# Letting any free flexible PSUM bank serve as the third bank of a ScalarE slot, and up to two VectorE jobs ride in one row-tiled score visit

## The chip, the cores and the metric

The kernel runs on one core of one Trainium2 chip. The metric is device time in microseconds (us); lower is better. Each timed run also lists the mean granted TensorE clock of the core (1.0 is full speed). Ratios are the mean time of one kernel's fast runs over the mean time of the other kernel's fast runs of the same rounds on the same chip, with a 95% interval. They are therefore not quite the ratios of the medians that are quoted beside them.

## The reference

A layernormed input goes through a 32-head softmax attention and through a gated unit, and the two are multiplied and added to the input:

```python
x = A_x                                      # (1, 2048, 640) bf16
xn = layernorm(x)
# attention, 32 heads of 20
q, k, v = split(xn @ wqkv)
p = softmax(einsum("bhqd,bhkd->bhqk", q, k) * 20 ** -0.5)
s = einsum("bhqk,bhkd->bhqd", p, v) @ wo
# gated unit, F = 1728
h = sigmoid(xn @ w_gate) * (xn @ w_up)
g = silu(h @ w_down)
return x + s * g
```

The attention has 32 x 2048 x 2048 scores. The kernel handles them as 2048 score tiles of 128 x 512 (8 groups of 4 heads, 4 query chunks, 16 key tiles, 4 heads each).

## The kernel before

A score tile needs an exponential. Two engines share that work. ScalarE takes most tiles, in "slots": two tiles lie in a two-bank PSUM tile (`scA`) and are done in one instruction, and a third may lie in a flexible bank (`bk`), as an instruction of its own. VectorE takes the others with integer arithmetic: one conversion per tile out of PSUM (`iv`), then three passes over a group of four tiles (`pb`). TensorE makes the scores in "visits" (heads of 20 rows are padded to 32 rows, a quarter of the array, so up to four score matmuls of different heads run at once; in the timeline below three start within 0.01 us), multiplies the finished tiles by V ("PV"), and fills the rest of its time with projections and the gated unit ("M"). Those M items need a flexible bank too. There are only three flexible banks.

All orders are fixed when the program is built. A small list scheduler with a clock of its own walks through time in steps of 0.02 us and decides what each engine issues next. On the chip every engine runs its list in order, so a late instruction holds up all that stands behind it (below, one output projection that waits 1.94 us holds up a score visit).

```python
# exponentials of a slot on ScalarE
m = len(jobs)
if m == SLOT:                                     # SLOT = 3
    flex[nexp % 2] = now + t_exp(1) + EL          # the slot's OWN flexible bank comes free
    exp_act(pt[:, 2, :], bank[nexp % 2])
exp_act(pt[:, 0:min(m, 2), :], scA[nexp % 2][:, 0:min(m, 2), :])
...
# a score visit on TensorE
d_bank, own = None, nfill % 2
if d_can and busy <= T_F + T_MODE + PL + SLACK:   # VectorE's backlog is small enough
    d_bank = next((f for f in [...][D_ORD] if flex[f] <= now), None)
want = SLOT if flex[nfill % 2] <= now and d_bank != nfill % 2 else SLOT - 1
... # at most one job for VectorE
jobs = claim_act(want, d_new[2][2] if d_new else None)
...
# output projections may start when a normalized block is expected to have landed
norm_b(*tm[1:])
o_at[tm[1]] = now + 11.5
```

## Time and profile before

Three runs took 839.08 to 841.6 us, median 841.25. The profiled run has a span of 839.8 us.

The first two lines below are from the profile's page of the kernel before: the busy time of each engine, and the granted TensorE clock in 40 slices of the span (9 is 90% or more). The next line is the chain of waits that ended last, by engine. The last two are groups of instructions (each shape apart): line, engine, operation, tiles, shapes and count, then busy time and mean ns of one, then the engine's idle time before them and what ended it.

```profile
PE 788.4 (94%) x6354; PEld 278.5 (33%) x6411; DVE 765.4 (91%) x1194; ACT 796.0 (95%) x1003; POOL 77.5 (9%) x84
...
PEclk9999999999999999999999999999999999999998
...
ACT 49%; PE 28%; DVE 13%; issue 6%; DMA 2%; SPq 1%; POOL 0%; POOLq 0%; ACTq 0%; DVEq 0%
...
L80 ACT ACTIVATE pt<-scA 128x1024 bf16<-128x1024 f32 x719 | 715.3, 1160 | 4.6 <-PE bk L860 2.9 <-PE scA L860 1.0
L80 ACT ACTIVATE pt<-bk 128x512 bf16<-128x512 f32 x129 | 94.5, 733 | 4.0 <-PE bk L860 3.8
```

Three engines are over 90% busy, so busy shares do not say who bounds the kernel. The chain does: ScalarE holds half of it. The mean of one exponential (1160 ns) is not its cost, because activations are pipelined and their records overlap.

The cost is the distance between starts. The next ScalarE instruction starts 903 ns after a 128x1024 exponential at best, 476 ns after a 128x512 one, 316 ns after a 128x320 tanh. Throughout this document, "ScalarE's sum" is all its instructions between the first and the last exponential times these best distances, and a "stall" is what a distance has above its best. (Four tanhs of 64x512 in each kernel are counted at 476 ns, though none takes under 612: 0.5 us of every kernel's stalls is this.) The stage from first to last exponential is the sum plus the stalls. (The prediction starts the stage one instruction later, at 34.0 us, hence its 777.6 and 754.2 us.)

| before | us |
|---|---|
| stage (33.5 to 811.7 us) | 778.1 |
| ScalarE's sum | 754.6 |
| stalls before 50 us / 50 to 755 us / after 755 us | 0.2 / 20.7 / 2.6 |
| behind the last exponential's start | 28.1 |

TensorE in the middle of the stage looks like this (timeline of the kernel before; columns are start, duration, engine, line, operation, tiles, shapes, count):

```profile
301.62 0.39 PE L860 MATMUL scA<-q,kT 32*128 32x512 bf16 x2
301.63 0.39 PE L860 MATMUL bk<-q,kT 32*128 32x512 bf16 x1
301.94 0.39 PE L897 MATMUL oacc<-pt,v 128*21 128x512 bf16 x2
301.95 0.39 PE L897 MATMUL oacc<-pb,v 128*21 128x512 bf16 x2
302.27 0.39 PE L641 MATMUL bk<-xnT,wgu 128*128 128x512 bf16 x1
302.60 0.39 PE L860 MATMUL scA<-q,kT 32*128 32x512 bf16 x2
302.60 0.39 PE L860 MATMUL bk<-q,kT 32*128 32x512 bf16 x1
```

A visit with two tiles for ScalarE and one for VectorE, one PV round, one M step and the next visit start about 0.32 us apart. Within one kind of work it is 0.213 us, so a change of kind costs about 0.107 us.

### The profile page before, as it was taken

How to read it: one execution, taken by the hardware profiler on the slowest of the kernel's cores; microseconds unless marked ns; L12 is line 12 of the kernel's file. 1: busy time of each engine (PE TensorE's matmuls, PEld its weight loads, DVE VectorE, ACT ScalarE, POOL GpSimd, SP SyncE). 2: the span in 40 equal slices, each digit the busy share in tenths (PEclk: the TensorE clock that was granted, in tenths of full speed). 3: DMA queues.
4: the chain of work that ended last, by engine and by line, in shares of the span. 5: the costliest groups of instructions: out<-in, count | busy, mean ns of one | idle time of the engine just before them, and what ended most of it. 6: DMA issues, size and time to landing. Idle time of an engine off the chain costs nothing.

```text
span 839.8 us, 16932 instructions
## 1 busy us (share of the span) xinstructions
PE 788.4 (94%) x6354; PEld 278.5 (33%) x6411; DVE 765.4 (91%) x1194; ACT 796.0 (95%) x1003; POOL 77.5 (9%) x84
## 2 busy tenths in 40 slices
PE   4799999999999999999999999999999999999995
PEld 2432323333333323333333233333233322333342
DVE  7789899999899998998999999999998988999994
ACT  7799999999999999999999999999999999999970
POOL 5000000000000001000000000000000000002333
PEclk9999999999999999999999999999999999999998
DMA  5711212123222132213121232131311223111642
GB/s 154 205 51 50 60 51 49 47 57 82 72 62 63 43 85 69 68 44 82 52 61 53 68 85 67 45 92 49 109 65 46 66 71 78 28 47 57 193 147 91
DMA packets 92979, 62.21 MB, mean 74 GB/s; under 512 B 34648, under 2 KB 86408, under 8 KB 92896
## 3 DMA queue, kind: packets, MB, share of 16 engines
q1 hardware_dynamic: 92608, 60.79, 25.7%
q8 instruction: 50, 0.82, 0.4%
q10 hardware_dynamic: 288, 0.33, 0.1%
q14 instruction: 33, 0.27, 0.1%
HBM read 46.24 MB, written 12.39 MB: 70 GB/s over the span
## 4 chain that ended last, share of the span: by engine, by line
ACT 49%; PE 28%; DVE 13%; issue 6%; DMA 2%; SPq 1%; POOL 0%; POOLq 0%; ACTq 0%; DVEq 0%
ACT pt L80 44%; PE scA L860 8%; PE oacc L897 5%; DVE iv L1194 5%; PE bk L679 4%; PE bk L641 3%; ACT tnh L80 3%; DVE pb L951 2%; PE bk L765 2%; PE bk L504 2%; DVE pb L945 1%; DVE pb L948 1%; DMA ld<-on 1%; PE psk L140 1%; ACT td L80 1%
## 5 line engine op out<-in xcount | busy, mean ns | idle before, releaser
L80 ACT ACTIVATE pt<-scA 128x1024 bf16<-128x1024 f32 (+1 forms) x729 | 720.2, 1153 | 4.6 <-PE bk L860 2.9
L1194 DVE TENSOR_SCALAR iv<-bk 128x512 int16<-128x512 f32 x471 | 318.6, 682 | 31.7 <-PE bk L860 30.2
L860 PE MATMUL scA<-q,kT 32*128 32x512 bf16 x1448 | 282.6, 382 | 16.7 <-ACT pt L80 9.6
L860 PE MATMUL bk<-q,kT 32*128 32x512 bf16 x600 | 215.5, 383 | 2.0 <-DVE iv L1194 1.7
L897 PE MATMUL oacc<-pt,v 128*21 128x512 bf16 x1577 | 183.1, 382 | 0.6 <-ACT pt L80 0.3
L860 PEld LDWEIGHTS <-kT 32*128 32x128 bf16 x2048 | 88.7, 91 | 261.6 <-issue 246.8
L897 PE MATMUL oacc<-pb,v 128*21 128x512 bf16 x942 | 152.9, 382 | 1.8 <-DVE on L910 1.5
L951 DVE TENSOR_TENSOR pb<-iv,pb 128x2048 bf16<-128x2048 bf16 x118 | 146.8, 1244 | 0.8
L641 PE MATMUL bk<-xnT,wgu 128*128 128x512 bf16 x471 | 142.6, 383 | 3.6 <-issue 1.7
L927 POOL TENSOR_TENSOR on_bf<-on,rl 128x512 bf16<-128x512 f32 x30 | 43.3, 1443 | 692.7 <-DMA rl<-rd 326.0
L80 ACT ACTIVATE pt<-bk 128x512 bf16<-128x512 f32 x129 | 94.5, 733 | 4.0 <-PE bk L860 3.8
L945 DVE TENSOR_SCALAR pb<-iv 128x2048 int16<-128x2048 int16 x118 | 86.3, 731 | 2.5
L679 PE MATMUL bk<-wd,hT 128*128 128x320 bf16 x448 | 86.9, 302 | 1.2 <-DVE iv L1194 0.7
L948 DVE TENSOR_SCALAR pb<-iv 128x2048 int16<-128x2048 int16 x118 | 82.6, 700 | 0.0
L897 PEld LDWEIGHTS <-v 128*21 128x21 bf16 x2519 | 50.4, 90 | 92.2 <-issue 69.4
L641 PEld LDWEIGHTS <-wgu 128*128 128x128 bf16 x520 | 37.1, 97 | 66.2 <-issue 50.4
L679 PEld LDWEIGHTS <-hT 128*128 128x128 bf16 x448 | 34.4, 97 | 48.4 <-issue 39.4
L504 PE MATMUL bk<-xnT,wu 128*120 128x512 bf16 x160 | 49.3, 399 | 0.4 <-DVE iv L1194 0.3
L80 ACT ACTIVATE tnh<-bk 128x512 bf16<-128x512 f32 (+1 forms) x56 | 41.6, 742 | 0.1
L649 DVE SCALAR_TENSOR_TENSOR hT<-tnh,bk 128x512 bf16<-128x512 bf16 x52 | 35.3, 680 | 5.9 <-PE bk L641 5.2
L612 PE MATMUL bk<-wv,xnT 128*128 128x160 bf16 x280 | 29.2, 234 | 0.7 <-ACT pt L80 0.6
L612 PEld LDWEIGHTS <-xnT 128*128 128x128 bf16 x280 | 18.6, 98 | 14.4 <-issue 14.1
(116 smaller groups left out, 381.3 us busy)
## 6 DMA issues: line engine op xcount, KB each, us to landing
wgu<-in_B_w_gate_dram SPq DMA_DIRECT2D x24, 320.0 KB
wgu<-in_B_w_up_dram SPq DMA_DIRECT2D x24, 320.0 KB
rl<-rd SPq DMA_DIRECT2D x120, 64.0 KB
gq_dram<-gqs SPq DMA_DIRECT2D x32, 160.0 KB
xnT<-gq_dram SPq DMA_DIRECT2D x12, 320.0 KB
xt<-in_A_x_dram SPq DMA_DIRECT2D x16, 160.0 KB
wd<-in_B_w_down_dram SPq DMA_DIRECT2D x1, 2080.0 KB
oU<-on_bf SPq DMA_DIRECT2D x104, 20.0 KB
```

Source lines behind the costliest of these rows:

```text
L80: return nc.scalar.add_instruction(mybir.InstActivation(func=func, name=nc.get_next_instruction_name(), engine=ENG.Activation, ins=[nc.sca ...
L504: nc.tensor.matmul(st["ps"][0:UC, :], lhsT=wus[u][:, kd, i, :], rhs=xnT[:, c, kd, :], start=(kd == 0), stop=(kd == KD - 1))
L612: nc.tensor.matmul(st["ps"][:, i * 2 * GC:(i + 1) * 2 * GC], lhsT=xn_tok(tts[i], kd), rhs=wvs[pr][:, kd, :], start=(kd == 0), stop=(kd == ...
L641: nc.tensor.matmul(st[key][0:fs, :], lhsT=w[:, i, kd, ko * P:ko * P + fs], rhs=xnT[:, c, kd, :], start=(kd == 0), stop=(kd == KD - 1))
L679: nc.tensor.matmul(st["ps"][:, 0:HD], lhsT=hT[0:fsz[kf], kf, t4 * P:(t4 + 1) * P], rhs=wd[0:fsz[kf], kf, h * HD:(h + 1) * HD], start=(kf = ...
L860: nc.tensor.matmul(dst, lhsT=kTs[(b // NQC) % 2][32 * j:32 * j + 32, kt * P:(kt + 1) * P], rhs=qts[b % 3][32 * j:32 * j + 32, :], start=Tr ...
L897: nc.tensor.matmul(oacc[32 * j:32 * j + DH + 1, :], lhsT=lhsT, rhs=u["src"], start=first, stop=last, tile_position=(0, 32 * j), skip_group ...
L927: nc.gpsimd.tensor_tensor(out=on_bf, in0=on, in1=rl, op=ALU.mult)
L945: nc.vector.tensor_scalar(out=pb[:, 0, :, :].bitcast(I16), in0=iv, scalar1=0x7F80, scalar2=1, op0=ALU.bitwise_and, op1=ALU.bitwise_or)
L948: nc.vector.tensor_scalar(out=pb[:, 1, :, :].bitcast(I16), in0=iv, scalar1=0x007F, scalar2=0x3F00, op0=ALU.bitwise_and, op1=ALU.bitwise_or)
L951: nc.vector.tensor_tensor(out=pb[:, 1, :, :], in0=iv.bitcast(BF16), in1=pb[:, 1, :, :], op=ALU.mult)
L1194: nc.vector.tensor_scalar(out=d["iv"][:, j, :], in0=bank[bk], scalar1=B_OFF, scalar2=0.0, op0=ALU.add, op1=ALU.max)
```

## The change

The intent is to make score visits fuller, so that TensorE needs fewer of them and changes its kind of work less often. Any free flexible bank may now be the third bank of a slot, and one visit may carry two VectorE jobs. Cut to its core:

```diff
+D_MAX, SLACKS = 2, (0.2, 0.2)
+A_BANKS, D_BANKS = ((0, 1, 2), (1, 0, 2)), ((2, 1, 0), (2, 1, 0))
+M_BANKS = ((2, 1, 0), (2, 1, 0))
...
-                                flex[nexp % 2] = now + t_exp(1) + EL
+                                flex[s["third"]] = now + t_exp(1) + EL
-                                exp_act(pt[:, 2, :], bank[nexp % 2])
+                                exp_act(pt[:, 2, :], bank[s["third"]])
...
-                    if d_can and busy <= T_F + T_MODE + PL + SLACK:
-                        d_bank = next((f for f in [...][D_ORD] if flex[f] <= now), None)
-                    want = SLOT if flex[nfill % 2] <= now and d_bank != nfill % 2 else SLOT - 1
+                    while len(d_new) < D_MAX and (dcur is not None or buf_free(iv_left, NIV)) \
+                            and busy + T_IV * len(d_new) <= T_F + T_MODE + PL + SLACKS[len(d_new)]:
+                        f = next((f for f in D_BANKS[own] if flex[f] <= now), None)
+                        ...                                    # claim a job for bank f
+                    third = next((f for f in A_BANKS[own] if flex[f] <= now), None) if len(d_new) < 2 else None
+                    jobs = claim_act(SLOT if third is not None else SLOT - 1, [y[2][2] for y in d_new])
```

(The line that prefers to wait 0.4 us for a bank and the bank order of M items were adapted too.) Because a scheduler sits between this and the program, the diff does not say what moves. The built orders of instructions do:

| | before | after |
|---|---|---|
| score visits / changes of TensorE's kind of work | 731 / 1530 | 691 / 1443 |
| exponentials of 128x1024 / in a third bank / 128x512 from scA | 719 / 129 / 10 | 686 / 210 / 2 |
| tiles on ScalarE / VectorE | 1577 / 471 | 1584 / 464 |
| PV visits | 665 | 670 |

More of the change, by code (lines that the diff above doesn't have):

```diff
@@ L840, in claim_act @@
             while len(got) < n:
-                js = [j for j in range(GH) if left[b][j] and j != not_j and all(x[2] != j for x in got)]
+                js = [j for j in range(GH) if left[b][j] and j not in not_j and all(x[2] != j for x in got)]
                 if not js:
@@ L848, in claim_act, with claim_dve @@
         return got
-    def claim_dve(had):
+    def claim_dve(had, not_j):
         for b in range(base(), min(NBLK, base() + 2)):
@@ L854, in claim_dve @@
             if n_left[b] >= (D_LAST if b < NBLK - 1 else D_LAST_END):
-                return take(b, max((j for j in range(GH) if left[b][j]),
-                                   key=lambda j: (j not in had, len(left[b][j]), j)), -1)
+                js = [j for j in range(GH) if left[b][j] and j not in not_j]
+                return take(b, max(js, key=lambda j: (j not in had, len(left[b][j]), j)), -1) if js else None
         return None
@@ L1249 @@
                         behind = done < due() + LAG
-                        for f in ((2,) if not behind and claimed[0] < NJOB * NBLK and not (FALL and not pv_ok and not can_f) else [(2, 1 - own, own), (2, own, 1 - own)][M_ORD]):
+                        for f in ((2,) if not behind and claimed[0] < NJOB * NBLK and not (FALL and not pv_ok and not can_f) else M_BANKS[own]):
                             if flex[f] <= now:
@@ L1268 @@
                     nxt = "PV"
-                elif can_f and (margin < URGENT or (stay is None and not (flex[nfill % 2] <= now + WAIT3 and flex[nfill % 2] > now and margin > WAIT3))):
+                elif can_f and (margin < URGENT or (stay is None and not (margin > WAIT3 and any(now < flex[f] <= now + WAIT3 for f in A_BANKS[nfill % 2]) and not any(flex[f] <= now for f in A_BANKS[nfill % 2])))):
                     nxt = "F"
@@ L1279 @@
                 if nxt == "F":
-                    d_can = dcur is not None or buf_free(iv_left, NIV)
                     busy = max(0.0, free["DVE"] - now) + T_IV * len(dq)
-                    d_bank, own = None, nfill % 2
-                    if d_can and busy <= T_F + T_MODE + PL + SLACK:
-                        d_bank = next((f for f in [(2, 1 - own, own), (2, own, 1 - own), (own, 2, 1 - own)][D_ORD] if flex[f] <= now), None)
-                    want = SLOT if flex[nfill % 2] <= now and d_bank != nfill % 2 else SLOT - 1
@@ L1286 @@
-                    d_new = None
-                    if d_bank is not None:
-                        x = claim_dve([t[2] for t in dcur["jobs"]] if dcur else [])
-                        if x is not None:
-                            if dcur is None:
-                                iv_left.append([1, 0.0])
-                                dcur = dict(jobs=[], n=0, k=0, i=len(iv_left) - 1,
-                                            iv=w2.tile([P, GH, QC], I16, tag="iv", bufs=NIV, name="iv"))
-                            d_new = dcur, len(dcur["jobs"]), x
-                            dcur["jobs"].append(x)
@@ L1296 @@
-                    jobs = claim_act(want, d_new[2][2] if d_new else None)
-                    if jobs or d_new is not None:
-                        for x, t in enumerate(jobs):
-                            score_mm(scA[nfill % 2][:, x, :] if x < 2 else bank[nfill % 2], *t)
-                        if d_new is not None:
-                            score_mm(bank[d_bank], *d_new[2])
-                            if len(dcur["jobs"]) == GH:
-                                dcur = None
+                    own = nfill % 2
@@ new lines @@
+                    d_new = []
+                    while len(d_new) < D_MAX and (dcur is not None or buf_free(iv_left, NIV)) \
+                            and busy + T_IV * len(d_new) <= T_F + T_MODE + PL + SLACKS[len(d_new)]:
+                        f = next((f for f in D_BANKS[own] if flex[f] <= now), None)
+                        if f is None:
+                            break
+                        x = claim_dve([t[2] for t in dcur["jobs"]] if dcur else [], [y[2][2] for y in d_new])
+                        if x is None:
+                            break
+                        if dcur is None:
+                            iv_left.append([1, 0.0])
+                            dcur = dict(jobs=[], n=0, k=0, i=len(iv_left) - 1,
+                                        iv=w2.tile([P, GH, QC], I16, tag="iv", bufs=NIV, name="iv"))
+                        d_new.append((dcur, len(dcur["jobs"]), x, f))
+                        dcur["jobs"].append(x)
+                        flex[f] = 1e9
+                        if len(dcur["jobs"]) == GH:
+                            dcur = None
@@ L1304 @@
+                    third = next((f for f in A_BANKS[own] if flex[f] <= now), None) if len(d_new) < 2 else None
+                    jobs = claim_act(SLOT if third is not None else SLOT - 1, [y[2][2] for y in d_new])
+                    if jobs or d_new:
+                        for x, t in enumerate(jobs):
+                            score_mm(scA[nfill % 2][:, x, :] if x < 2 else bank[third], *t)
                         end = now + T_F + (T_MODE if mode != "F" else 0.0)
-                        if d_new is not None:
-                            dq.append((d_new[0], d_new[1], d_bank, end + PL))
-                            flex[d_bank] = 1e9
+                        for d, i, x, f in d_new:
+                            score_mm(bank[f], *x)
+                            dq.append((d, i, f, end + PL))
@@ L1310 @@
                             if len(jobs) == SLOT:
-                                flex[nfill % 2] = 1e9
+                                s["third"] = third
+                                flex[third] = 1e9
                             nfill += 1
```

## The prediction

> **What bounds the kernel now.** The page gives busy shares of 95% ScalarE (796.0 us), 94% TensorE (788.4) and 91% VectorE (765.4), which alone names no winner. The chain of waits does: 49% of it is ScalarE, 44% the exponentials alone. I read the starts of successive ScalarE instructions in the trace. A 128x1024 exponential is followed after 903 ns at best, a third-bank 128x512 one after 476 ns. From the first exponential (34.0 us) to the last (811.7 us) are 777.6 us; instructions times their best interval give 754.2 us. So ScalarE issues 97% of the stage, and only 23.5 us are stalls (some 85 of 60 ns or more, the rest jitter). The list of waits shows under 8 us of them. The same count gives VectorE 706 us of work in the stage and 96 us of stall: it has room. Behind ScalarE's end come about 27 us of output projection and stores.
>
> **What the change does**, by the order of instructions of the built kernels:
> - Score visits 731 to 691; matmuls are 2048 in both. Visits with three ScalarE jobs rise from 129 to 210; 49 visits carry two VectorE jobs.
> - Changes of TensorE between kinds of work 1530 to 1443, PV visits 665 to 670.
> - ScalarE: 128x1024 exponentials 719 to 686, third-bank ones 129 to 210, 128x512 from scA 10 to 2. It takes 1584 of the 2048 score tiles instead of 1577.
> - VectorE: 7 fewer bank conversions, 116 groups of three passes instead of 118.
>
> **Costs.** TensorE: starts in the trace are 0.213 us apart within a kind and about 0.32 us across a change, so a change costs about 0.107 us. (The Trainium skill, "TensorEngine Tiling (Array Packing)", Key Properties, says that changing the tiling mode drains TensorE; the trace agrees with a change costing this 0.107 us.) Estimate: -40 x 0.213 + 5 x 0.213 - 87 x 0.107 = -17 us of TensorE work. VectorE: about -8 us. ScalarE: 81 x 0.476 - 33 x 0.903 - 8 x 0.477 = **+4.9 us**, since a third bank is an instruction of its own (two jobs in one instruction cost 0.903, two separate ones 0.952) and seven more tiles land there.
>
> **On the critical path.** Only ScalarE's line counts nearly fully. TensorE's 17 us pay only by making scores arrive earlier: at most the 23.5 us of stalls, less 4.9 added, so 18.6 us (2.2%) is the ceiling. Fewer, larger slots (1.38 us instead of 0.90 per slot) give TensorE more time per refill. I expect stalls to fall from 23.5 to about 13 us: -10.5 + 4.9 = about -5.6 us, and nothing much in the head and tail. That gives 841.25 - 5.6, **about 835.5 us, range 828 to 842**. Chances: faster by over 2% 0.04, within 2% 0.95, slower by over 2% 0.01.
>
> **What the profile would show.**
> - Right: ScalarE stage from first to last exponential near 772 us; its best-interval sum 759 us; stalls of 60 ns and more fewer than 85; TensorE busy at least 10 us below 788; VectorE busy about 757 us; ScalarE still the largest share of the chain.
> - Third-bank exponentials 210, still 476 ns.
> - Wrong: stage still 778 us or more with stalls unchanged.
>
> **What would make it wrong.** (1) Stalls come not from TensorE's load but from buffers or from GLU items whose tanh must follow matmuls: then only +4.9 us remains and the kernel is 0.5% slower. (2) Third banks held by ScalarE and paired VectorE jobs starve the misc. matmuls of banks, which then pile up in the tail. (3) Two VectorE jobs at once make VectorE late with `hT` or bank releases. (4) Stalls nearly vanish: 826 us.

## The result, and the profile after

Four runs took 843.42 to 845.78 us, median 844.75, beside 840.77 for the kernel before (four runs, 839.08 to 841.6). The ratio is 1.004 (1.0016 to 1.0063): within 2%, but slower, where a gain of 0.7% had been forecast. The result is correct.

The lines of the page and the groups that answer to those shown of before (kernel after; its lines stand 3 lower in the file):

```profile
PE 788.9 (94%) x6404; PEld 279.6 (33%) x6404; DVE 757.7 (90%) x1180; ACT 800.3 (95%) x1043; POOL 78.4 (9%) x85
...
PEclk9899999999999999999999999999999999998998
...
ACT 54%; PE 22%; DVE 12%; issue 7%; DMA 2%; SPq 2%; POOL 1%; POOLq 0%; DVEq 0%; ACTq 0%
...
L83 ACT ACTIVATE pt<-scA 128x1024 bf16<-128x1024 f32 x686 | 706.0, 1179 | 6.8 <-PE bk L863 5.1 <-PE scA L863 1.0 <-PE oacc L900 0.4
L83 ACT ACTIVATE pt<-bk 128x512 bf16<-128x512 f32 x210 | 155.9, 742 | 2.4 <-PE bk L863 2.1
```

The counts are as the order said, and ScalarE's share of the chain grew. The best distances are unchanged (903 and 476 ns). Two new things stand in the clock line: slices below 9 near 21 to 42 us and near 758 to 779 us. The trace lists three half-clock windows inside the stage: 6.8 us from about 34 us, and 3.4 us each from about 765 and 771 us. The profiled run before has none inside the stage.

| | before | after |
|---|---|---|
| stage | 778.1 | 783.0 |
| ScalarE's sum | 754.6 | 759.6 |
| stalls before 50 / 50 to 755 / after 755 us | 0.2 / 20.7 / 2.6 | 2.0 / 16.7 / 4.7 |
| all stalls | 23.5 | 23.4 |
| behind the last exponential's start | 28.1 | 26.2 |

ScalarE's sum rose by 5.0 us, as forecast. The stalls did not fall. The middle of the stage gave 4 us, and its two ends took them back. That is what the prediction had named as the sign of being wrong: "stage still 778 us or more with stalls unchanged".

Where the late stalls are, the timeline shows (kernel after, TensorE; the bracket is idle time before the instruction and what ended it):

```profile
766.31 0.61 PE L863 MATMUL scA<-q,kT 32*128 32x512 bf16 x2 [0.26 <-ACT pt L83]
766.32 0.60 PE L863 MATMUL bk<-q,kT 32*128 32x512 bf16 x1
766.86 1.22 PE L768 MATMUL bk<-wo,oU 128*128 128x320 bf16 x4
770.02 0.30 PE L768 MATMUL bk<-wo,oU 128*128 128x320 bf16 x1 [1.94 <-DMA oU<-on_bf]
770.25 0.39 PE L863 MATMUL scA<-q,kT 32*128 32x512 bf16 x2
```

And ScalarE over the same time (timeline of the kernel after):

```profile
767.08 0.59 ACT L83 ACTIVATE pt<-bk 128x512 bf16<-128x512 f32 x1
767.55 1.03 ACT L83 ACTIVATE pt<-scA 128x1024 bf16<-128x1024 f32 x1
770.74 1.02 ACT L83 ACTIVATE pt<-scA 128x1024 bf16<-128x1024 f32 x1 [2.15 <-PE bk L863]
771.66 0.59 ACT L83 ACTIVATE pt<-bk 128x512 bf16<-128x512 f32 x1
```

TensorE started an output projection whose fifth input had not landed yet. The score visit that ScalarE needed stood behind it, and ScalarE's next start came 2.28 us late. Before the wait the matmuls are 0.6 us long instead of 0.39: that is the half clock.

How busy TensorE was shows in a table of windows (columns: window and its length, then busy us and count of PE, PEld, DVE, ACT, POOL, then PEclk, DMA share, GB/s). First the kernel before:

```profile
50.00:755.00 705.00, 680.55 (x5488) 231.38 (x5540) 658.17 (x1000) 699.57 (x866) 40.11 (x28) 1.00 0.23 62
755.00:812.00 57.00, 55.34 (x463) 20.49 (x463) 54.29 (x86) 56.25 (x68) 15.44 (x16) 1.00 0.40 126
```

The same windows of the kernel after:

```profile
50.00:755.00 705.00, 684.15 (x5565) 235.46 (x5565) 651.84 (x989) 703.06 (x902) 39.69 (x28) 1.00 0.23 63
755.00:812.00 57.00, 50.88 (x427) 17.36 (x425) 51.98 (x83) 53.65 (x68) 16.11 (x16) 0.94 0.43 129
```

After 755 us TensorE is busy for 50.88 us instead of 55.34, and it is there that the clock falls to 0.94. In the long middle the freed work is not visible as idle time: one matmul's record is about 0.38 us long while starts are 0.213 us apart, so records cover small gaps. (In this profile of before, some matmul records are missing: 5488 against 5540 weight loads.) The prediction's test "TensorE busy at least 10 us below 788" was a poor one: 44 us of work left out in a later run (light_undone) lower this busy time from 680.55 to 655.25 us, by 25 us only.

### The profile page after: what moved, and what is told of

It is laid out like the page before. It is cut to its first block, busy times and chain, and to the rows that moved or that the text cites. A ratio compares the mean times of both kernels' runs of the same rounds, so it can differ in the third digit from the quotient of the medians.

```text
span 841.7 us, 16978 instructions
## 1 busy us (share of the span) xinstructions
PE 788.9 (94%) x6404; PEld 279.6 (33%) x6404; DVE 757.7 (90%) x1180; ACT 800.3 (95%) x1043; POOL 78.4 (9%) x85
## 4 chain that ended last, share of the span: by engine, by line
ACT 54%; PE 22%; DVE 12%; issue 7%; DMA 2%; SPq 2%; POOL 1%; POOLq 0%; DVEq 0%; ACTq 0%
ACT pt L83 48%; PE scA L863 6%; PE bk L644 4%; PE oacc L900 4%; DVE iv L1197 4%; ACT tnh L83 2%; DVE pb L954 2%; PE bk L682 2%; DVE pb L951 2%; PE bk L768 1%; DVE pb L948 1%; ACT td L83 1%; PE bk L615 1%; PE bk L507 1%; DVE hT L652 1%
## 5 line engine op out<-in xcount | busy, mean ns | idle before, releaser
L83 ACT ACTIVATE pt<-scA 128x1024 bf16<-128x1024 f32 (+1 forms) x688 | 707.0, 1178 | 6.8 <-PE bk L863 5.1
L1197 DVE TENSOR_SCALAR iv<-bk 128x512 int16<-128x512 f32 x464 | 312.3, 681 | 40.2 <-PE bk L863 37.7
L863 PE MATMUL scA<-q,kT 32*128 32x512 bf16 x1374 | 269.6, 384 | 18.3 <-ACT pt L83 12.5
L900 PE MATMUL oacc<-pt,v 128*21 128x512 bf16 x1584 | 188.6, 385 | 0.3 <-ACT pt L83 0.2
L863 PEld LDWEIGHTS <-kT 32*128 32x128 bf16 x2048 | 86.1, 91 | 259.1 <-issue 243.4
L83 ACT ACTIVATE pt<-bk 128x512 bf16<-128x512 f32 x210 | 155.9, 742 | 2.4 <-PE bk L863 2.1
L900 PE MATMUL oacc<-pb,v 128*21 128x512 bf16 x928 | 149.2, 383 | 1.5 <-DVE pb L954 1.0
L644 PE MATMUL bk<-xnT,wgu 128*128 128x512 bf16 x520 | 145.8, 382 | 1.7 <-DVE iv L1197 0.8
L954 DVE TENSOR_TENSOR pb<-iv,pb 128x2048 bf16<-128x2048 bf16 x116 | 144.1, 1242 | 0.5
L768 PE MATMUL bk<-wo,oU 128*128 128x320 bf16 (+1 forms) x120 | 24.2, 314 | 1.9 <-DMA oU<-on_bf 1.9
```

The source lines that it names most:

```text
L83: return nc.scalar.add_instruction(mybir.InstActivation(func=func, name=nc.get_next_instruction_name(), engine=ENG.Activation, ins=[nc.sca ...
L644: nc.tensor.matmul(st[key][0:fs, :], lhsT=w[:, i, kd, ko * P:ko * P + fs], rhs=xnT[:, c, kd, :], start=(kd == 0), stop=(kd == KD - 1))
L863: nc.tensor.matmul(dst, lhsT=kTs[(b // NQC) % 2][32 * j:32 * j + 32, kt * P:(kt + 1) * P], rhs=qts[b % 3][32 * j:32 * j + 32, :], start=Tr ...
L900: nc.tensor.matmul(oacc[32 * j:32 * j + DH + 1, :], lhsT=lhsT, rhs=u["src"], start=first, stop=last, tile_position=(0, 32 * j), skip_group ...
L954: nc.vector.tensor_tensor(out=pb[:, 1, :, :], in0=iv.bitcast(BF16), in1=pb[:, 1, :, :], op=ALU.mult)
L1197: nc.vector.tensor_scalar(out=d["iv"][:, j, :], in0=bank[bk], scalar1=B_OFF, scalar2=0.0, op0=ALU.add, op1=ALU.max)
```

## The experiments

Four theories were tried against each other. Theory 1: ScalarE's sum sets the stage and the stalls stay near 23 us whatever TensorE has to do. Theory 2, the prediction's: the stalls follow TensorE's load. Theory 3: windows of half TensorE clock cost the changed kernel time. Theory 4: a wait that the fixed order did not foresee (the DMA of `oU`) costs it time. In the tables, stalls are before 50 / 50 to 755 / after 755 us. "Before" ran beside them with medians of 842.49, 842.07, 841.25 and 841.45 us in the four jobs.

### Undoing all, and each half alone

```diff
 # undone
-D_MAX, SLACKS = 2, (0.2, 0.2)
-A_BANKS, D_BANKS = ((0, 1, 2), (1, 0, 2)), ((2, 1, 0), (2, 1, 0))
-M_BANKS = ((2, 1, 0), (2, 1, 0))
+D_MAX, SLACKS = 1, (0.2, 0.2)
+A_BANKS, D_BANKS = ((0,), (1,)), ((2, 0, 1), (2, 1, 0))
+M_BANKS = ((2, 1, 0), (2, 0, 1))
 # third_only: only D_MAX = 1
 # pair_only:  only A_BANKS = ((0,), (1,))
 # slack04:    only SLACKS = (0.4, 0.2)
```

> The changed code with all of its new settings put back (own bank only, one VectorE job, old bank orders): every engine's instruction order is that of the kernel before, so the time must be equal within 0.1% (841 us). It is a null test and shows how the TensorE clock of the old order behaves over several runs. Theory 3 (the loss comes from windows of half clock that the changed kernel happens to run into) expects a mean clock near 0.997 here in every run, against 0.986 to 0.989 in the four runs of the changed kernel. Theories 1 and 2 say nothing about the clock; if the clocks here spread over 0.986 to 0.997 too, theory 3 loses its ground.

> Only the first half of the change: any free bank may be the third bank; one VectorE job a visit. By the order of instructions: 673 score visits, 1407 changes of TensorE, 260 third-bank exponentials, ScalarE takes 1600 tiles, VectorE 448. Theory 1 (ScalarE's own issue time sets the stage, stalls stay near 23 us whatever TensorE's load): ScalarE's sum is 13.5 us above before, so about 853 to 855 us, ratio 1.015. Theory 2 (my prediction's: stalls follow TensorE's load, and 58 visits and 123 changes fewer are some 25 us less of it): stalls fall by 10 us or more, so 845 us or less. Theory 3: near 841 us unless the clock falls.

> Only the second half: up to two VectorE jobs a visit; third bank the slot's own as before. 734 score visits, 1522 changes of TensorE, 117 third-bank exponentials, ScalarE takes 1573 tiles. Theory 1: ScalarE's sum falls by 2.2 us, stalls as before: 838.5 to 839.5 us. Theory 2: TensorE's load is unchanged, so the stalls are too: also 839. Theory 3: as the clock falls out. It tells which half of the change carries the loss.

> The changed kernel with one number changed: a first VectorE job is given out while VectorE's backlog exceeds the visit by up to 0.4 us instead of 0.2 us. ScalarE takes 1566 tiles (18 fewer than the changed kernel), third-bank exponentials 160, score visits 707, changes of TensorE 1481. Theory 1: ScalarE's sum is 9.3 us under the changed kernel and 4.3 us under before: about 836 us. Theory 2: TensorE has more to do than in the changed kernel (16 visits, 38 changes), so stalls grow: 842 us or more.

| | median us | ratio to before (95%) | ScalarE's sum | stalls | stage |
|---|---|---|---|---|---|
| undone | 841.69 | 0.9999 (0.9981 to 1.0016) | 754.6 | 1.9 / 19.6 / 1.9 | 778.1 |
| third_only | 854.08 | 1.0145 (1.0125 to 1.0164) | 768.5 | 0.2 / 19.4 / 5.2 | 793.2 |
| pair_only | 838.51 | 0.9962 (0.9943 to 0.9981) | 752.4 | 0.0 / 21.3 / 1.5 | 775.3 |
| slack04 | 839.44 | 0.9967 (0.9947 to 0.9986) | 750.3 | 3.0 / 18.2 / 1.3 | 772.8 |

The null test holds. The flexible third bank alone loses 1.45%, where theory 1 said 1.5% and theory 2 half a per cent or less, although it has the fewest visits of the four. It is the loss-making half: VectorE gets 448 tiles instead of 471, and the missing 23 tiles land on ScalarE. The likely reason, that a third bank held for ScalarE is not there for VectorE, was not tested apart from the lower number of visits (673 instead of 731, with at most one VectorE job each). The pair of VectorE jobs alone gains 0.4% as forecast. (Both halves keep the changed kernel's order of banks for VectorE and M.) In slack04 the stage fell by 5.3 us with the sum (-4.3), but the time behind the last exponential grew from 28.1 to 32.5 us, so the median is 3.4 us above the 836 of theory 1. Three of its six runs had a clock of 0.990 and took 840.7 to 840.8 us, the two at 0.997 took 837.2 and 837.9.

The clock half of the expectation for undone failed: its clocks were 0.990 to 0.995, and those of before ranged from 0.990 to 0.997 in that job. So the old order has half-clock windows too (6.8 us from about 34 us in undone's profile), only fewer. They go with time: over the four jobs of experiments, runs of before at a clock of 0.997 averaged 840.8 us (11 runs), those at 0.992 or less 842.8 us (13 runs). These pool four chips, so only the size is meant.

third_only has still more half-clock windows (table of windows, the same two stretches):

```profile
50.00:755.00 705.00, 675.33 (x5441) 234.56 (x5484) 632.37 (x951) 701.44 (x920) 38.23 (x28) 0.99 0.24 66
755.00:812.00 57.00, 48.32 (x392) 14.71 (x390) 49.97 (x76) 54.23 (x69) 12.69 (x13) 0.87 0.25 72
```

After 755 us, TensorE's busy time of 55.3, 50.9 and 48.3 us in before, after and third_only goes with a clock of 1.00, 0.94 and 0.87. That less work makes the windows is suggested by this, not shown. The Trainium skill, "TensorE: Matmul & The Clock Gate", Part 1, says that the array's clock is halved after at least one idle window of about 3.4 us and that this window runs free of the kernel. The traces agree in size (3.4, 6.8 and 10.2 us at half clock) and in chance (the window near 34 us comes in some runs of one kernel and not in others). But the stretches ahead of the windows were not empty. These are the 3.4 us ahead of the two late windows of the kernel after (they reach 0.3 us into the windows, hence the clock of 0.96), and those ahead of a window that light_after, below, had at 502 us:

```profile
761.40:764.80 3.40, 2.04 (x22) 0.69 (x21) 3.08 (x6) 3.40 (x6) 0.96 (x1) 0.96 0.88 282
768.20:771.60 3.40, 1.58 (x17) 0.50 (x17) 1.36 (x3) 1.25 (x2) 0.67 (x1) 0.96 0.05 12
498.70:502.10 3.40, 2.89 (x15) 0.94 (x14) 3.11 (x5) 3.40 (x6) 0.00 (x0) 1.00 0.15 39
```

TensorE was busy in them for 2.04, 1.58 and 2.89 us of 3.40, and the clock was halved all the same. In the long middle of the stage the kernel after is busy for 97% (684.15 of 705 us) and keeps its clock; light_undone, below, is busy for 93% (655.25 us) and keeps it too. No share of busy time that holds the clock comes out of these records.

What a window costs comes out clearly before 50 us, over all 16 profiles. In the eight without a half-clock window there, ScalarE's stalls before 50 us are 0.0 to 0.2 us; with 3.4 us of it (two profiles) they are 1.0 to 1.1, with 6.8 us (three) 1.9 to 2.0, with 10.2 us (three) 2.7 to 3.1 us. So about 0.3 us of ScalarE's time is lost there for each us at half clock, whichever kernel it is.

### The clock and the wait for the DMA

```diff
 # warm: matmuls whose result nobody reads
 def s_bound(eng):
+    warm = psP.tile([P, KD, P], BF16, tag="tp", ...)...bitcast(FP32)
+    for i in range(7):
+        nc.tensor.matmul(warm, lhsT=ident, rhs=xnT[:, 0, i % KD, 0:KD * P // 2], start=True, stop=True)
 ...
+elif nxt is None and cur is None and base() >= 26 and ... warm_gap() > 0.32 + ... and any(flex[f] <= now for f in range(3)):
+    nc.tensor.matmul(bank[f], lhsT=ident, rhs=xnT[:, NQC - 1, 0, :], start=True, stop=True)   # 12 of them; 13 in warm_oat15, 2 in undone_both
 # oat15
-o_at[tm[1]] = now + 11.5
+o_at[tm[1]] = now + 15.0
 # warm_oat15: both.  undone_warm: undone and the 7 matmuls.
```

> The changed kernel plus matmuls whose result nobody reads, only to keep TensorE busy: 7 of 320 columns in TensorE's idle time just before the first score visit, and 12 of 512 columns in planned idle gaps from block 26 on (about 690 us). ScalarE takes 1585 tiles, its sum is that of the changed kernel within 0.3 us. Theory 3 (half-clock windows cost the changed kernel 2 to 3 us more than the kernel before: 13.7 us of them fell into the stage in its profile): windows at 34 us and after 745 us go or shrink, clock 0.993 or more, 841 to 842.5 us, ratio to before about 1.000. Theory 1 alone (ScalarE's sum plus a constant 23 us of stalls): no gain, 844 to 845 us, ratio 1.004.

> The old order of instructions (as in undone) plus only the 7 unread matmuls before the first score visit. Over 11 runs of the old order the time fell from about 843 us at a clock of 0.991 to 840.4 at 0.997. Theory 3: the window near 34 us goes, clock 0.995 to 0.997 in every run, median 840 to 840.8, ratio 0.998. If the window near 34 us costs nothing, or TensorE's idle time does not bring it, ratio 1.000 and clocks spread as before.

> The changed kernel, with the plan told that a normalized block lands 15.0 us after its start instead of 11.5, so that output projections are placed later. ScalarE's sum is 0.6 us lower (1583 tiles). In the changed kernel's profile TensorE stood 1.94 us at one output projection, waiting for the DMA of oU, and ScalarE's next slot came 2.28 us late. Theory 4 (a wait that the fixed TensorE order did not foresee, with all later work behind it): that wait is gone, the stage from first to last exponential is about 2.5 to 3 us shorter (780 us), but the projections move to the end, so the total may gain only 0 to 2 us. Theory 1 alone: stage shorter by 0.6 us.

> Both of the last two edits of the changed kernel together. Theories 3 and 4 together: stage 777 to 779 us against 783.0, stalls of ScalarE near 18 us instead of 23.4, total 840 to 842 us. Theory 1 alone: stage 782 to 783 us, total 844 us.

| | median us | ratio to before (95%) | ScalarE's sum | stalls | stage |
|---|---|---|---|---|---|
| warm | 844.47 | 1.0025 (1.0004 to 1.0046) | 760.0 | 0.0 / 16.6 / 4.3 | 780.9 |
| undone_warm | 841.59 | 1.0000 (0.9980 to 1.0020) | 754.6 | 1.0 / 19.8 / 2.6 | 778.1 |
| oat15 | 845.09 | 1.0043 (1.0021 to 1.0065) | 759.1 | 2.7 / 17.6 / 2.8 | 782.2 |
| warm_oat15 | 841.22 | 0.9988 (0.9971 to 1.0005) | 759.2 | 2.0 / 16.1 / 1.3 | 778.5 |

Two of the four expectations failed. undone_warm is a miss: seven matmuls did not remove the early window (3.4 us of it remained in the profile), and nothing was gained. warm missed its 841 to 842.5 us: the windows near 34 and 765 us were gone from its profile (the early one by chance, perhaps: warm_oat15 has the same seven matmuls and 6.8 us of it), but TensorE's wait for the DMA of `oU` only moved, to about 793 us (1.6 us), with a half-clock window of 3.4 us beside it. oat15 lost that wait, but kept windows near 768 and 774 us, moved projections behind the last exponential (29 us there instead of 26), and gained nothing.

Together the two edits did what neither did alone: the late stalls fall from 4.7 to 1.3 us, the stage is 778.5 us (777 to 779 expected), and the ratio falls from 1.004 to 0.999, although the time behind the last exponential grew from 26.2 to 28.8 us. The unread matmuls are not the whole of warm_oat15's effect: with both edits the scheduler also chose a slightly different order (1583 tiles on ScalarE instead of 1584).

TensorE's longest waits, as the list of waits has them (who waited for whom: us in total, times, longest), first in warm_oat15:

```profile
PE scA L866 <- ACT pt L83: 12.6, 43, 1.0
PE tp L281 <- DVE xn L274: 11.0, 3, 10.0
PE psk L143 <- ACT xnT L284: 2.3, 3, 1.1
```

and then in the changed kernel, run once more (after_again, below):

```profile
PE scA L863 <- ACT pt L83: 12.9, 41, 1.0
PE tp L281 <- DVE xn L274: 10.8, 2, 10.4
PE bk L768 <- DMA oU<-on_bf: 1.9, 1, 1.9
```

The wait for the DMA of `oU` is in the second list and not in the first.

### The changed kernel again, the same edits on the old order, and the other direction

```diff
 # after_again: the changed kernel, unedited.  undone_both: undone with the edits of warm_oat15
 # no_third
-D_MAX, SLACKS = 2, (0.2, 0.2)
-A_BANKS = ((0, 1, 2), (1, 0, 2))
+D_MAX, SLACKS = 1, (0.2, 0.2)
+A_BANKS = ((), ())
 # slack04_b
-SLACK = 0.2;  SLACKS = (0.2, 0.2)
+SLACK = 0.1;  SLACKS = (0.4, 0.2)
```

> The changed kernel itself once more, on the chip of the next three runs and in more rounds: ratio to before 1.003 to 1.005, 845 us, clock 0.986 to 0.990. In its profile again a wait of some 2 us of TensorE for the DMA of oU near 770 us and half-clock windows after 745 us, if those are the kernel's own and not chance of one run.

> The old order with the two edits that together brought the changed kernel from 1.004 to 0.999 (unread matmuls, of which only 2 fall into late gaps here, and output projections placed later). The kernel before has neither the DMA wait nor late half-clock windows. Theories 3 and 4 (both are costs that the change brought in): nothing to gain here, ratio 0.999 to 1.002. If the edits are a general gain: ratio 0.995.

> The other direction: no third bank at all, one VectorE job a visit. Order of instructions: 789 score visits, 1627 changes of TensorE, 785 exponentials of two tiles or one, ScalarE takes 1564 tiles: ScalarE's sum is 9.1 us under before (about 745.5 us) and TensorE's load some 22 us above it by the same unit costs as in the prediction. Theory 1 (ScalarE's sum plus a constant 23 us): 832 us. Theory 2 (stalls follow TensorE's load): stalls of 40 us or more, 855 us or more. A result in the second range would mean that stalls do follow the load once it is above that of the kernel before, and that only below it nothing is left to win.

> The changed kernel with VectorE backlog allowed to 0.4 us for the first job (as in slack04) and the bank conversion's preference over a pass cut from 0.2 to 0.1 us. ScalarE takes 1557 tiles, its sum is 8.5 us under before and 13.4 under the changed kernel. Theory 1: 832 to 834 us, ratio 0.991. If the stalls that the plan itself holds grow by as much as ScalarE's sum falls, as its order suggests: 838 to 840 us, ratio 0.997, no better than slack04.

| | median us | ratio to before (95%) | ScalarE's sum | stalls | stage |
|---|---|---|---|---|---|
| after_again | 843.92 | 1.0034 (1.0010 to 1.0059) | 759.6 | 0.0 / 16.1 / 5.5 | 781.2 |
| undone_both | 842.00 | 1.0005 (0.9990 to 1.0020) | 755.6 | 0.2 / 18.7 / 1.7 | 776.2 |
| no_third | 857.23 | 1.0185 (1.0149 to 1.0222) | 745.5 | 0.1 / 32.1 / 3.5 | 781.2 |
| slack04_b | 838.22 | 0.9959 (0.9945 to 0.9973) | 746.6 | 0.1 / 21.9 / 2.4 | 770.9 |

after_again repeats the loss, the wait of 1.9 us, and a half-clock window of 10.2 us from 763 us. These two costs belong to the changed kernel and are not the chance of one run. The same edits on the old order gain nothing, so they are no general improvement: they mend what the change brought in.

no_third went the way of theory 2: with 789 visits instead of 731 its stalls are 12 us longer and eat the 9 us that ScalarE's sum loses. Its time behind the last exponential also grew, to 35 us from 28. The 855 us or more came true in the median; the stalls of 40 us or more did not show in the profile (35.7 us), which is of the fastest of four runs (851.59 to 861.84 us, clocks 0.997 to 0.987). Its stalls end theory 1's constant 23 us. But this run changes two things at once, TensorE's load and the depth of the slots (two tiles at most, so 0.90 us per refill and never 1.38), which is why two more runs were made.

slack04_b is faster than both kernels: 0.9959 beside 1.0034 for the changed kernel in the same rounds. It is no better than pair_only or slack04 by more than their intervals. Its sum is 8.0 us under before and its stage 7.2 us; 0.9 us went into stalls. Another 2.4 us were lost behind the last exponential (30.5 us against 28.1), and the median of 838.22 is over 4 us above what theory 1 said. The other branch of the expectation had the right time (838 to 840 us) for the wrong reason: it wanted stalls to grow by as much as the sum falls.

### TensorE's load alone

```diff
 # light_after and light_undone: wrong result on purpose, every other instruction in its place
 def mm(key, i, kd):
     w = wgu_tiles[(c, k2)]
+    if kd in (2, 3):
+        return                     # 208 of 520 gate and up matmuls left out
     nc.tensor.matmul(st[key][0:fs, :], ...)
```

> The changed kernel with 208 of its 520 full gate and up matmuls left out (two of five in each group; the result is wrong on purpose), nothing else moved: ScalarE and VectorE keep every instruction and its place, TensorE loses 208 x 0.213 = 44 us of work. If TensorE's work ahead of score visits makes ScalarE's stalls (theory 2): stalls between 50 and 755 us fall from 16.5 us to below 9, since TensorE now runs ahead. If they come from elsewhere (slots, banks, VectorE): 14 us or more stay. Total 832 to 845 us accordingly; the wait for the DMA of oU near 770 us stays or grows.

> The same 208 matmuls left out of the old order (wrong on purpose). Theory 2: stalls between 50 and 755 us from about 20 to below 11 us. Otherwise 17 us or more stay. If here and in light_after the same rest remains, that rest is not TensorE's, and the prediction's ceiling (all 23.5 us may go) was too high by it.

| | median us | ratio to before (95%) | ScalarE's sum | stalls | stage |
|---|---|---|---|---|---|
| light_after | 846.35 | 1.0058 (1.0031 to 1.0084) | 759.6 | 3.1 / 17.3 / 5.6 | 785.6 |
| light_undone | 841.63 | 1.0011 (0.9996 to 1.0027) | 754.6 | 1.1 / 19.4 / 2.3 | 777.4 |

TensorE lost 208 x 0.213 = 44 us of work and ScalarE's stalls in the middle did not move: 17.3 instead of 16.7 and 16.1 us, and 19.4 instead of 19.6 us. What moved is who waits for whom. These are TensorE's longest waits in light_undone:

```profile
PE scA L865 <- ACT pt L83: 35.6, 118, 0.7
PE tp L281 <- DVE xn L274: 10.9, 3, 10.0
```

and in the kernel before:

```profile
PE tp L278 <- DVE xn L271: 10.5, 2, 10.1
PE scA L860 <- ACT pt L80: 9.6, 40, 0.5
```

TensorE now waits 35.6 us for ScalarE to free its slots, against 9.6 before. Taking work from TensorE gave TensorE idle time and gave ScalarE nothing. In light_after the wait for the DMA of `oU` grew to 2.9 us, the clocks were 0.984 to 0.987, and the median of 846.35 lies above the 832 to 845 us expected.

So, at least from the load of the old order downwards, the stalls are not made by how much TensorE has to do. One candidate that is left is where single score visits stand in its order. In the trace of the kernel before, 74 stalls of over 60 ns lie between 50 and 755 us (17.3 us). For 62 of them (14.9 us) the score visit that ScalarE waited for had started right behind other TensorE work (PV, gate and up, down) and ScalarE followed within 620 ns of the visit's start. In the kernel after there are 48 such stalls with 9.6 us. ("Right behind" means that the matmul before the visit had started at most 360 ns earlier; in nine of the 62 that one is a score matmul itself.) But by the same test some 79% of all score visits in this stretch start right behind other work (567 of 718, beside 62 of 74), so this count does not single them out as the cause.

The traces hold a better lead. Sort the stalls between 50 and 755 us by the slot that ScalarE worked off just before (with the 64x512 tanh at its own 612 ns). In the kernel before, 540 slots follow one of at most two tiles and have 19.0 us of stalls (35 ns each); 117 follow one of three tiles and have 1.1 us (10 ns each). In the kernel after they are 434 with 14.4 us (33 ns) and 187 with 1.8 us (10 ns). The cost for a slot hardly changed, but the mix did, and an estimate from the costs of before puts this at about -3 us (106 x 35 ns less, 70 x 10 ns more). That is the prediction's other reason, "Fewer, larger slots (1.38 us instead of 0.90 per slot) give TensorE more time per refill", and no_third, with 31.6 us in 706 slots after at most two tiles, fits it. It remains a correlation: the scheduler gives a third tile only when a bank is free, third_only fits less well (226 slots after three tiles with 23 ns each), and no run changed the depth alone.

## Why the prediction was wrong

**Right.** ScalarE bounds the stage; it held 54% of the chain afterwards. The ScalarE term was +4.9 us and measured +5.0 (759.6 against 754.6). Third-bank exponentials are 210 at 476 ns. VectorE busy was forecast at about 757 us and is 757.7. The time behind the last exponential was forecast as unchanged and fell by 1.9 us.

**Wrong, and decisive: "I expect stalls to fall from 23.5 to about 13 us".** The term of -10.5 us measured -0.1 us in the first profile and -1.9 us in the second. The runs split it in three.

1. In the middle of the stage the stalls fell by about 4 us (from 20.7 to 16.7 and 16.1). With the undone runs as the reference (19.6 to 19.8) it is about 3.3. The prediction let TensorE's 17 us of freed work, and larger slots, take 10 us off. The step that failed is the first: freed work was to make scores arrive earlier, and light_after and light_undone show that by itself it buys none: 44 us of it moved nothing. What fits the small drop is the second, the other mix of slots, at about 3 us; that was not isolated. My ceiling, "at most the 23.5 us of stalls", was no estimate of what could be had.
2. After 755 us stalls rose by 2.1 to 2.9 us. TensorE, with less to do, stood at an output projection whose DMA was not there (1.9 us, in both profiles), with score visits behind it, and its clock was halved around that wait. Warning (2) of the prediction, work that piles up in the tail for want of banks, did not come true: the time behind the last exponential fell.
3. Before 50 us a half-clock window took 2.0 us in the first profile and nothing in the second. The old order meets it too (1.9 us in undone).

The sum for the first profile: +5.0 ScalarE, -4.0 middle, +2.1 late, +1.8 early, -1.9 behind the last exponential and -1.0 before the first one make +2.0; the spans differ by 1.9 us. The medians of all runs differ by 4.0 and 2.7 us. The profiled run after was the fastest of its four, and the others had lower clocks (0.986 to 0.988).

**The prediction's own alternative (1)** said that if the stalls do not come from TensorE's load, only the +4.9 us remains and the kernel is 0.5% slower. That is nearly what was measured (0.3 to 0.4%), and the load runs show the first half of its premise to be true (not TensorE's load); "buffers" or the tanhs as the source were not shown. That the number comes near is partly luck: it foresaw +4.9 us alone, and beside this term stand -4.0 us in the middle, +3.9 us at the stage's two ends and -2.9 us before and behind it. It was given too little weight: the upper end of the range, 842 us, left it out.

**What the two halves did.** The flexible third bank costs 1.45% by itself, because it moves tiles from VectorE to ScalarE, the engine that bounds (23 tiles at half of 0.903 us are 10 of the 13.9 us that the sum grew). The pair of VectorE jobs gains 0.4% by itself. The change as a whole is the first paid back in part by the second.

**Open.** How the remaining 16 us of stalls in the middle, mostly under 250 ns each, divide over single places in TensorE's order was not tried one by one, nor was the depth of the slots changed alone. How much of the late cost is the wait and how much the clock no run separates cleanly. The profiles allow an estimate: late stalls are 4.7 us in the changed kernel (wait and 6.8 us at half clock), 2.8 in oat15 (6.8 us at half clock, no wait) and 1.3 in warm_oat15 (neither), so some 1.9 us for the wait and 1.5 for the clock, from single profiles whose orders differ a little. (The prediction's 706 us of work and 96 of stall for VectorE add up to more than the 777.6 us stage, so they cannot both be right; nothing above rests on them.)

## What to carry to other kernels

When one engine issues 97% of its stage, price a change first by what it adds to or takes from that engine; the ratios of the two halves followed that sum to about 0.2%. (no_third did not: its sum fell by 9 us and it lost 1.85%, so look at the stalls when the depth of the slots changes.) Work taken from a neighbour with a fixed order turns into that neighbour's waiting, not into earlier results: test it by leaving work out with the order kept, before crediting it with a gain. A changed fixed order can also meet a DMA that the old one did not have to wait for, so look at the longest single waits of the feeding engine before and after.

## What the Trainium skill lacked or had wrong

- "TensorE: Matmul & The Clock Gate", Part 1, has the clock halved after an idle window, and further on tells of a kernel whose clock oscillates because TensorE idles briefly and often between groups of matmuls. For that second case it gives no size of how much idle time is enough. Here the clock was halved after 3.4 us in which TensorE's records show 2.04, 1.58 and 2.89 us busy. Runs of the old order at a mean clock of 0.997 and of 0.992 or less differed by about 2 us (840.8 and 842.8, pooled over four chips).
- "TensorEngine Tiling (Array Packing)", Key Properties, says that changing the tiling mode drains TensorE but gives no size. Here a change between row-tiled scores, column-tiled PV and whole-array matmuls costs about 0.107 us (starts 0.32 us apart instead of 0.213).
